# Two 64-row halves of the matmul array side by side in a fused attention and gated-MLP kernel

## The chip, the core and the metric

The kernel runs on one core of one Trainium2 chip. The metric is the device time of one execution in microseconds (us). Three executions of the kernel before gave 696.16, 697.24 and 698.26 us; their median is 697.24 us.

## The reference

```
xn  = layernorm(x)                                   # x: 2048 x 448
out = x + A(xn) @ wo + (sigmoid(xn @ w_gate) * (xn @ w_up)) @ w_down    # 448 -> 1792 -> 448
A: 16 heads of 28 channels, 4 segments of 512 tokens; in each segment causal
   softmax(q k^T / sqrt(28)) v, mixed by sigmoid(beta) with a memory
   phi(q) M / phi(q) z, where M and z are summed over the segments before
```

Everything is fp32. The kernel keeps the accuracy by splitting an operand into a high part, rounded to the matmul's format (float32r), and a low part, the remainder, and by adding the products high x high, high x low and low x high.

## The kernel before

The 448 channels are held in chunks of 128 rows: three whole chunks and a tail of 64. `xs[b]` holds the normalised tokens of block b (512 tokens) as seven slices of 128 partitions by 512 tokens: slices 0 to 2 the high parts of the three whole chunks, 4 to 6 their low parts, and slice 3 the tail, the 64 channels' high part in partitions 0 to 63 and their low part in partitions 64 to 127. A weight tile has eight slices of the same kind, its slices 3 and 7 holding the tail's high and low parts, each twice. `TERMS` (line 53) lists the eleven pairs of slices whose products make one output: nine for the whole chunks, two for the tail.

A front part (to about 165 us) normalises the tokens and computes keys, queries, values and the memory. Then one long loop does two things at once, and its PE order is written out by hand (`manual_schedule` for PE and SP): generators yield after a few matmuls, and the driver at the end (lines 766 to 779) draws one step of attention for a fixed number of steps of the MLP.

- The MLP (`gated`, line 159) walks over 14 groups f of 128 hidden channels, two at a time, and for each pair over the four token blocks: 56 blocks (f, b). A block computes the gate product and the up product, eleven matmuls of 128x512 each (line 240, output `pgu`), then ACT takes tanh of the gate (line 248, output `sg`), DVE multiplies it with the up product (line 249), ACT writes the high half of the result (line 251, `hh`) and DVE the low half (line 252). Between these, the down products of the block two steps back (`down`, line 161, output `pd`) are issued for two tiles of 128 tokens, six matmuls of 448 columns each (line 166), and DVE adds them to `acc` (line 169).
- Attention works on 32 pairs of heads. `scores` (line 588) makes for each pair five PSUM banks of scores (line 597, output `st`), one attention step each; the rows of an operand are 84, three times 28, since the high and low parts are stacked. ACT copies each bank to `w` in SBUF (lines 601 and 604), POOL masks the diagonal tiles (line 612), DVE takes maxima (lines 614 and 618, output `mx`). `weights` (line 624) then finishes a pair: small DVE maxima and POOL copies between partitions (lines 628 to 638), a DVE transpose that spreads the maximum (line 641, `mb`), and three times a DVE subtraction (line 651) and an ACT exponential (line 652). After two pairs, `finish` multiplies the weights with the values (line 672, output `pa`, 128x32 tiles) and DVE normalises (lines 675 to 678).

The eight PSUM banks have tags (line 113): two `p`, two `s`, one `m`, two `gu`, one `pd`. The gate product uses `gu`, the up product `p`, the down products `pd` and `gu` in turn, the scores `s` in turn. A product that opens a bank has to wait until the engine that read the bank's last content is done. The order on ACT, DVE and POOL in this loop is not written by hand: the framework's scheduler lays it out when the program is built, and each of these engines then works strictly through its list.

Of the kernel before, what the change touches and what calls it, by code (L numbers as in the profile page):

```python
# [2 lines left out]

# [6 lines left out]
F32 = mybir.dt.float32  # L10
# [28 lines left out]
SLOT = (0, 0, 0, None, 0, 0, 2, 3, 1, 1, 1, None, 1, 1)  # L39
# [14 lines left out]
KS = 3 * DH  # L54
# [7 lines left out]
def kernel(  # L62
# [96 lines left out]
    def gated():  # L159

        def down(b, hs, wd, t, tag="pd"):
            tok = slice(t * P, (t + 1) * P)
            mms = [(h[:, a, tok], wd[f][:, w, :]) for f, h in hs for a, w in ((0, 0), (0, 1), (1, 0))]
            pd = bank("pd", tag)
            for n, (l, r) in enumerate(mms):
                T.matmul(pd[:, :D], l, r, start=n == 0, stop=n == len(mms) - 1)  # L166
                if n == 2:
                    yield
            V.tensor_add(acc[b][:, t, :], pd[:, :D], acc[b][:, t, :])  # L169
            yield  # L170
# [37 lines left out]
        todo = [None, None]  # L208
        for f0 in range(0, NF, FG):
# [22 lines left out]
            for b in range(NB):  # L232
                hs = []
                for f in range(f0, f0 + FG):
                    pgu = []
                    for side in range(2):
                        slot = 2 * (f - f0) + side
                        dst = bank("pgu", ("gu", "p")[side])
                        for n, (a, w) in enumerate(TERMS):
                            T.matmul(dst, wgu[f][:, w, side * P:(side + 1) * P], xs[b][:, a, :],  # L240
                                     start=n == 0, stop=n == len(TERMS) - 1)
                            if n in (3, 7):
                                yield
                        pgu.append(dst)
# [10 lines left out]
                        yield  # L255
                        if todo and f0 + b > 0:
                            yield from todo.pop(0) or ()
# [3 lines left out]
                todo += [down(b, hs, wdn, t, ("pd", "s" if end else "gu")[t % 2]) for t in range(NT)]  # L261
        rest.extend(todo)
# [305 lines left out]
    class Pair:  # L568
# [5 lines left out]
        def load(self):  # L574

            self.qk = sb.tile([P, 2, 2, L], F32R, name="qk2", bufs=2)
            for c, parts in enumerate(((0, 0), (1, 0), (0, 1))):
                for n in range(2):
                    r0 = D * (1 - n) + DH * self.h0
                    nc.sync.dma_start(self.qk[DH * c:DH * (c + 1), n].bitcast(F32),  # L580
                                      qd[self.s][r0:r0 + 2 * DH, parts[n], :].rearrange("(j p) f -> p j f", p=DH))
# [6 lines left out]
        def scores(self):  # L588
# [4 lines left out]
            for n in range(5):  # L593
                st = bank("st", "s")
                for h, kb in (((n // 2, 0),), ((n // 2, 1), (n // 2, 3)))[n % 2] if n < 4 else ((0, 2), (1, 2)):
                    at = KB[kb] % L + (256 * h if kb == 2 else 0)
                    T.matmul(st[:, at:at + L - kb * P], self.qk[:KS, 1, h, kb * P:(kb + 1) * P],  # L597
                             self.qk[:KS, 0, h, kb * P:], start=True, stop=True)
                if n < 4:
                    w = self.w[:, HW * (n // 2) + L * (n % 2):][:, :L]  # L600
                    A.activation(w, st, AF.Copy)  # L601
                else:
                    w = w3[:, :, 2 * L:]
                    A.activation(w, st.rearrange("p (h n) -> p h n", h=2), AF.Copy)

                if n % 2 == 0 and n < 4:
                    d = w[:, :P]
                    pattern = [[1, P]]
                else:
                    d = w.rearrange("p (a n) -> p a n", n=P)[:, 0:4:3, :] if n < 4 else w[:, :, :P]  # L610
                    pattern = [[0, 2], [1, P]]
                G.affine_select(d, d, pattern=pattern, base=0, channel_multiplier=-1, compare_op=ALU.is_ge, fill=MASK)  # L612
                if n in (1, 3):
                    V.tensor_reduce(mx[:, 16 * (n - 1):16 * (n + 1)],  # L614
                                    w3[:, n // 2, :2 * L].rearrange("p (b n) -> p b n", n=32),
                                    axis=mybir.AxisListType.X, op=ALU.max, apply_transpose=True)
                if n == 4:
                    V.tensor_reduce(mx[:, 64:80].rearrange("p (h b) -> p h b", h=2),
                                    w.rearrange("p h (b n) -> p h b n", n=32),
                                    axis=mybir.AxisListType.X, op=ALU.max, apply_transpose=True)  # L620
                yield
# [112 lines left out]
    def project():  # L734
# [11 lines left out]
        for n in range(NB * NT + 2):  # L746
# [5 lines left out]
            if n >= 2:  # L752
# [10 lines left out]
                if rest:  # L763
                    yield from rest.pop(0)
# [54 lines left out]
```

## Time and profile before

| | |
|---|---|
| median of three runs | 697.24 us |
| the profiled execution's own time | 699.29 us |
| its span, first to last instruction | 697.6 us |
| PE busy | 690.0 us (99%), 3594 matmuls |
| DVE busy | 570.2 us (82%) |
| ACT busy | 343.6 us (49%) |
| POOL busy | 148.5 us (21%) |
| mean granted TensorE clock | 0.997 |

PE is the matmul engine and PEld its weight loads, which run beside the matmuls. A duration of a matmul runs from its start to its modelled end and overlaps the next one; what a matmul costs in a row of matmuls is read from the chain that ended last, where a piece is a time and a count. "idle before" names the engine or DMA that a waiting instruction was released by.

### The profile page before, as it was taken

The numbers are of one execution on the slowest core, as the hardware profiler recorded it, in microseconds if no ns is written. First come the engines' busy times: TensorE is split into PE (matmuls) and PEld (weight loads), VectorE is DVE, ScalarE is ACT, GpSimd is POOL, SyncE is SP. The second block draws the span as 40 slices with busy tenths as digits, with TensorE's granted clock in tenths as the row PEclk, the third lists the DMA queues.
The fourth block names the chain that finished last, engine by engine and source line by source line (L and its number), as shares of the span: only waits on it lengthen the run. The fifth ranks groups of instructions, "written<-read, shape, count | busy, mean of one in ns | idle before, by whom it ended". The sixth has DMA issues, their size and how long they took to land.

```text
span 697.6 us, 10438 instructions
## 1 busy us (share of the span) xinstructions
PE 690.0 (99%) x3594; PEld 567.7 (81%) x3594; DVE 570.2 (82%) x994; ACT 343.6 (49%) x563; POOL 148.5 (21%) x349
## 2 busy tenths in 40 slices
PE   8989999999999999999999999999999999999997
PEld 7878878777878787877878778787787878778897
DVE  6665687658789898988898889998898889889863
ACT  5646646344455455543655446455644555446320
POOL 4400010101222131322222222132221322222000
PEclk9999999999999999999999999999999999999999
DMA  7833545687222423234323343324242432333342
GB/s 265 320 130 149 201 185 211 226 300 224 70 77 65 120 86 85 48 113 108 78 58 96 70 128 66 98 56 114 74 108 66 95 70 60 86 94 88 91 152 105
DMA packets 45797, 84.37 MB, mean 121 GB/s; under 512 B 6321, under 2 KB 20401, under 8 KB 45233
## 3 DMA queue, kind: packets, MB, share of 16 engines
q1 hardware_dynamic: 42736, 76.37, 35.3%
q0 software_dynamic: 3008, 7.34, 5.2%
q8 instruction: 28, 0.46, 0.3%
q14 instruction: 25, 0.20, 0.1%
HBM read 51.05 MB, written 32.64 MB: 120 GB/s over the span
## 4 chain that ended last, share of the span: by engine, by line
PE 94%; DMA 2%; DVE 1%; ACT 1%; SPq 0%; issue 0%; ACTq 0%
PE pgu L240 42%; PE pd L166 20%; PE pp L344 9%; PE st L597 5%; PE pa L672 5%; PE po L756 5%; PE pv L326 4%; PE pmm L372 2%; PE n L390 1%; DMA qd<-qk 1%; DMA acc<-in_x 1%; PE pt L95 1%; PE pk L364 1%; DVE stats L285 0%; ACT L512 0%
## 5 line engine op out<-in xcount | busy, mean ns | idle before, releaser
L240 PE MATMUL pgu<-xs,wgu 128*128 128x512 f32 x1232 | 321.0, 398 | 0.0
L240 PEld LDWEIGHTS pgu<-xs,wgu 128*128 128x128 f32 x1232 | 226.6, 188 | 48.0 <-issue 3.2
L166 PE MATMUL pd<-wdn,hh 128*128 128x448 f32 x672 | 162.4, 368 | 0.0
L612 POOL TENSOR_SCALAR_AFFINE_SELECT w<-w 128x256 f32<-128x256 f32 (+1 forms) x160 | 81.7, 512 | 254.1 <-ACT w L601 215.1
L166 PEld LDWEIGHTS pd<-wdn,hh 128*128 128x128 f32 x672 | 123.2, 188 | 15.1 <-issue 1.0
L652 ACT ACTIVATE w<-w 128x1024 f32<-128x1024 f32 (+1 forms) x96 | 87.1, 915 | 87.6 <-DVE w L651 87.0
L651 DVE TENSOR_TENSOR w<-w,mb 128x1024 f32<-128x1024 f32 (+1 forms) x96 | 99.7, 1049 | 0.2
L601 ACT ACTIVATE w<-st 128x512 f32<-128x512 f32 x128 | 75.0, 588 | 43.6 <-PE st L597 43.5
L614 DVE TRANSPOSE_TENSOR_REDUCE mx<-w 128x32 f32<-128x1024 f32 x64 | 79.1, 1235 | 12.7 <-POOL w L612 12.7
L344 PE MATMUL pp<-xs,wqk 128*128 128x512 f32 x308 | 80.6, 412 | 0.0
L344 PEld LDWEIGHTS pp<-xs,wqk 128*128 128x128 f32 x308 | 58.1, 192 | 14.8 <-issue 2.4
L169 DVE TENSOR_TENSOR acc<-pd,acc 128x448 f32<-128x448 f32 x112 | 67.4, 602 | 2.7 <-PE pd L166 2.5
L597 PE MATMUL st<-qk 84*128 84x128 f32 (+3 forms) x256 | 64.0, 311 | 0.0
L251 ACT ACTIVATE hh<-sg 128x512 fp32r<-128x512 f32 x56 | 35.1, 627 | 44.5 <-DVE sg L249 35.0
L597 PEld LDWEIGHTS st<-qk 84*128 84x128 f32 x256 | 48.4, 189 | 8.6 <-ACT w L601 0.2
L248 ACT ACTIVATE sg<-pgu 128x512 f32<-128x512 f32 x56 | 33.3, 594 | 40.1 <-PE pgu L240 40.1
L641 DVE STREAM_TRANSPOSE mb<-top 128x1024 f32<-128x1024 f32 x32 | 39.8, 1242 | 10.3 <-POOL top L638 10.1
L351 DVE TENSOR_TENSOR qk<-pp,qk 128x512 fp32r<-128x512 f32 x28 | 19.3, 688 | 34.6 <-ACT e L349 27.3
L249 DVE SCALAR_TENSOR_TENSOR sg<-sg,pgu 128x512 f32<-128x512 f32 x56 | 37.4, 668 | 4.8 <-PE pgu L240 4.8
L252 DVE SCALAR_TENSOR_TENSOR hh<-sg,hh 128x512 fp32r<-128x512 f32 x56 | 38.6, 690 | 2.7 <-ACT hh L251 2.5
L326 PE MATMUL pv<-wv,xs 128*128 128x448 f32 x176 | 39.7, 377 | 0.3
L672 PE MATMUL pa<-w,vv 128*32 128x128 f32 (+3 forms) x512 | 38.4, 436 | 0.0
(100 smaller groups left out, 639.2 us busy)
## 6 DMA issues: line engine op xcount, KB each, us to landing
qk<-qd SPq DMA_DIRECT2D x192, 112.0 KB
qd<-qk SPq DMA_DIRECT2D x28, 512.0 KB
raw<-in_w_ffn SPq DMA_DIRECT2D x14, 512.0 KB
vd<-vst SPq DMA_DIRECT2D x4, 1024.0 KB
vv<-vd SPq DMA_DIRECT2D x16, 256.0 KB
od<-w POOLq DMA_DIRECT2D x16, 256.0 KB, 4.0
sums<-od SPq DMA_DIRECT2D x32, 128.0 KB
out<-acc SPq DMA_DIRECT2D x16, 224.0 KB
```

What stands on the lines that cost most here:

```text
L166: T.matmul(pd[:, :D], l, r, start=n == 0, stop=n == len(mms) - 1)
L169: V.tensor_add(acc[b][:, t, :], pd[:, :D], acc[b][:, t, :])
L240: T.matmul(dst, wgu[f][:, w, side * P:(side + 1) * P], xs[b][:, a, :], start=n == 0, stop=n == len(TERMS) - 1)
L326: T.matmul(pv[:, :D], xs[b][:, a, t * P:(t + 1) * P], wv[w], start=n == 0, stop=n == len(TERMS) - 1)
L344: T.matmul(pp, wqk[c][:, w, :], xs[b][:, a, :], start=n == 0, stop=n == len(TERMS) - 1)
L597: T.matmul(st[:, at:at + L - kb * P], self.qk[:KS, 1, h, kb * P:(kb + 1) * P], self.qk[:KS, 0, h, kb * P:], start=True, stop=True)
L601: A.activation(w, st, AF.Copy)
L612: G.affine_select(d, d, pattern=pattern, base=0, channel_multiplier=-1, compare_op=ALU.is_ge, fill=MASK)
L614: V.tensor_reduce(mx[:, 16 * (n - 1):16 * (n + 1)], w3[:, n // 2, :2 * L].rearrange("p (b n) -> p b n", n=32), axis=mybir.AxisListType.X, ...
L651: V.tensor_sub(w, w, m)
L652: A.activation(w, w, AF.Exp, scale=SCALE)
L672: T.matmul(pa[32 * j:32 * j + 32, kb * P:], self.vv[:, kb, 32 * j:32 * j + 32], self.pairs[j // 2].block(j % 2, kb), start=kb == 0, stop=k ...
```

## The change

All products of the loop use the array as two tiles of 64 rows by 128 columns. The new helper `half_by_half` takes two outputs in two PSUM banks. In a first way, rows 0 to 63 add to output 0 and rows 64 to 127 to output 1, one matmul of each in turn; in a second way the outputs change places. Before the second way stands a `keepalive_nop` on PE that names both outputs, so PE waits for the first way's last matmuls to have finished. Other work is issued between the two ways.

```diff
+HALF = [slice(0, 64), slice(64, P)]
+CROSS = [t for c in range(3) for t in ((c, c), (c, 4 + c), (4 + c, c))]
+EARLIER, LATER = slice(0, L // 2), slice(L // 2, L)
+ENDS = [[(EARLIER, 3, 3), (LATER, 3, 3), (EARLIER, 3, 7)], [(LATER, 3, 3), (EARLIER, 3, 3), (LATER, 3, 7)]]
+KS = 3 * DH // 2
...
-        V.tensor_sub(dst[64:, 3, tok], p3[64:, 3], dst[64:, 3, tok].bitcast(F32))
+        low = HALF[1 - t // 2]
+        V.tensor_sub(dst[low, 3, tok], p3[low, 3], dst[low, 3, tok].bitcast(F32))
...
+    def half_by_half(outs, steps, part):
+        for way in range(2):
+            todo = [steps((r + way) % 2, r) for r in range(2)]
+            count = max(len(s) for s in todo)
+            for n in range(count):
+                for r in range(2):
+                    if n < len(todo[r]):
+                        cols, stationary, moving = todo[r][n]
+                        T.matmul(outs[(r + way) % 2][:, cols], stationary, moving, start=way == 0 and n == 0,
+                                 stop=way == 1 and n == len(todo[r]) - 1)
+                if n % part == part - 1 and n < count - 1:
+                    yield
+            yield
+            if way == 0:
+                T.keepalive_nop([T.lower_ap(o[0:1, 0:1]) for o in outs])
...
+            if halves:
+                pds = [bank("pd", t) for t in ("pd", tag)]
+                mms = half_by_half(pds, lambda o, r: steps(o, HALF[r]), 3)
+                for n in range(4):
+                    next(mms)
+                    if n == 3:
+                        add(0)
+                        add(1)
                     yield
...
+        def gate_up(f, xb, pgu):
+            def steps(o, r):
+                return [(tok, wgu[f][HALF[r], w, o * P:(o + 1) * P], xb[HALF[r], a, tok])
+                        for tok, a, w in [(slice(None), a, w) for a, w in CROSS] + ENDS[r]]
+            yield from half_by_half(pgu, steps, 4)
...
-            for n in range(5):
-                st = bank("st", "s")
...
+            for n, kbs in enumerate(((0,), (1, 3), (2,))):
+                st = [bank("st", "s") for _ in range(2)]
...
+                mms = half_by_half(st, steps, 2)
+                next(mms)
+                yield
+                next(mms)
+                w = w3[:, :, L * n:min(L * (n + 1), HW)]
+                for h in range(2):
+                    A.activation(w[:, h], st[h][:, :w.shape[2]], AF.Copy)
```

The tail changes with it: in the second half of a block's 512 tokens the low part now lies in partitions 0 to 63 and the high part in 64 to 127. So each half of the array needs three tail products of 256 columns per output (`ENDS`) where two of 512 columns on all rows stood. Per output and way there are nine products of 512 columns and three of 256.

Gate and up products of a block now run as one unit: both outputs in the first way, then two steps of the down products (their first way), then the second way, then two steps of the down products (their second way). The two tiles of 128 tokens of a down product are made together, and both adds follow at the end. Three of the 56 blocks, the first three, and the last three pairs of down tiles keep the old form. The scores of both heads of a pair are made together: three groups of two banks (512; 384 and 128; 256 columns), each in two ways, each way an attention step; a pair so has six steps instead of five and two empty steps of a unit are gone (`SLOT`). ACT copies two banks per group, 192 copies instead of 160, and POOL has 128 masks instead of 160. The operands of the scores are loaded as 28 and 14 rows into each half of the partitions, by eight DMAs per pair instead of six (256 instead of 192).

The built program has 3263 matmul instructions before and 5533 after. On ACT, DVE and POOL the scheduler has laid out the rest anew. On ACT, from the last score copy (L604) of a pair of heads, w_2463, in the before; `L652` are this pair's exponentials, `L248` tanh of a gate, `w_2589` the next pair's scores:

```order
L604 ACTIVATE w_2463<-st_2550 128x2x256
L601 ACTIVATE w_2589<-st_2591 128x512
L601 ACTIVATE w_2589<-st_2612 128x512
L251 ACTIVATE hh_2603<-sg_2600 128x512
L601 ACTIVATE w_2589<-st_2634 128x512
L248 ACTIVATE sg_2681<-pgu_2627 128x512
L652 ACTIVATE w_2463<-w_2463 128x2x512
L652 ACTIVATE w_2463<-w_2463 128x2x2x256
```

Between a pair's last score copy and its first exponential stood five entries: three score copies of the next pair, an `hh` and a tanh. The same place of the same pair (the sixth) on ACT in the after; `L678` are score copies, `L725` exponentials, `L313` tanh:

```order
L678 ACTIVATE w_2861<-st_2982 128x256
L678 ACTIVATE w_2861<-st_2981 128x256
L725 ACTIVATE w_2861<-w_2861 128x2x512
L725 ACTIVATE w_2861<-w_2861 128x2x2x256
L313 ACTIVATE sg_3067<-pgu_2963 128x512
L725 ACTIVATE w_2861<-w_2861 128x2x2x128
L678 ACTIVATE w_3053<-st_3056 128x512
```

The exponentials now follow the score copies at once, and the next tanh and score copies stand behind them. On DVE at the same place before, from the last of that pair's small maxima to its second subtraction (L651); `L249` and `L252` belong to the MLP, `L169` is an add of down products:

```order
L636 TENSOR_TENSOR top_2582<-mx_2464,up_2581 32x32
L641 STREAM_TRANSPOSE mb_2610<-top_2582 128x1024
L249 SCALAR_TENSOR_TENSOR sg_2600<-sg_2600,pgu_2569 128x512
L169 TENSOR_TENSOR acc0_69<-pd_2606,acc0_69 128x448
L614 TENSOR_REDUCE mx_2590<-w_2589 128x32
L252 SCALAR_TENSOR_TENSOR hh_2603<-sg_2600,hh_2603 128x512
L651 TENSOR_TENSOR w_2463<-w_2463,mb_2610 128x2x512
L651 TENSOR_TENSOR w_2463<-w_2463,mb_2610 128x2x2x256
```

And on DVE in the after (`L691` the last maximum, `L714` the transpose, `L724` the subtractions, `L314` the multiplication with the up product):

```order
L691 TENSOR_REDUCE mx_2862<-w_2861 128x16
L703 TENSOR_TENSOR mx_2862<-mx_2862 128x2x8
L707 TENSOR_TENSOR mx_2862<-mx_2862,up_3045 64x2x16
L709 TENSOR_TENSOR top_3046<-mx_2862,up_3045 32x32
L714 STREAM_TRANSPOSE mb_3080<-top_3046 128x1024
L724 TENSOR_TENSOR w_2861<-w_2861,mb_3080 128x2x512
L724 TENSOR_TENSOR w_2861<-w_2861,mb_3080 128x2x2x256
L724 TENSOR_TENSOR w_2861<-w_2861,mb_3080 128x2x2x128
L314 SCALAR_TENSOR_TENSOR sg_3067<-sg_3067,pgu_2964 128x512
```

The MLP's entries that stood between the transpose and the subtractions have moved behind them. On PE in the after, from the last score products of that pair to the gate product that opens the bank which the tanh above reads (the row of eight is its beginning; a count of two is one matmul on each half):

```order
L129 MATMUL st<-qk_2552 128x256 x2
L129 MATMUL pd<-wdn,hh 128x448 x6
L129 MATMUL pgu<-xs_67,wgu 128x512 x16
L129 MATMUL st<-qk_2749 128x512 x2
L129 MATMUL pgu<-xs_67,wgu 128x512 x2
L129 MATMUL pgu<-xs_67,wgu 128x256 x6
L129 MATMUL pd<-wdn,hh 128x448 x6
L129 MATMUL st<-qk_2749 128x512 x2
L129 MATMUL pd<-wdn,hh 128x448 x6
L129 MATMUL pgu<-xs_67,wgu 128x512 x8
```

On PE in the before, from the same pair's last score products on:

```order
L597 MATMUL st<-qk_2253 128x256 x2
L166 MATMUL pd<-wdn,hh 128x448 x3
L240 MATMUL pgu<-xs_67,wgu 128x512 x8
L597 MATMUL st<-qk_2383 128x512
L240 MATMUL pgu<-xs_67,wgu 128x512 x3
L166 MATMUL pd<-wdn,hh 128x448 x3
L597 MATMUL st<-qk_2383 128x384
L597 MATMUL st<-qk_2383 128x128
L166 MATMUL pd<-wdn,hh 128x448 x3
L240 MATMUL pgu<-xs_67,wgu 128x512 x4
```

Before, groups of scores used the two `s` banks in turn; now both banks of a group are opened, read and opened again together, and the same holds for the `pd` and `gu` banks of a pair of down tiles.

More of the change, by code (lines that the diff above doesn't have):

```diff
@@ L254, in gated @@
                             hs.append((f, hh))
-                        yield
-                        if todo and f0 + b > 0:
-                            yield from todo.pop(0) or ()
+                        if between:
+                            for _ in range(2):
+                                next(between)
+                                yield
+                        else:
+                            yield
                         if (b, slot) in ahead:
@@ L260, in gated @@
                 end = f0 + FG == NF and b == NB - 1
[L261 to L262 removed]
+                todo += [partial(down, b, hs, wdn, t, "s" if end else "gu") for t in (0, 2)]
+        rest.extend(d(False) for d in todo)
     N_FFN = NF // FG * NB * 20 - 12
@@ L763, in project @@
                 if rest:
-                    yield from rest.pop(0)
+                    for _ in range(2):
+                        next(rest[0])
+                        yield
+                    if n % 2 == 1:
+                        rest.pop(0)
     N_OUT = 1 + NB * NT * 3 + 12
```

98 lines of the change are left out of this document (54 added, 44 removed).

## The prediction

> **What bounds the kernel now.** I read the page's busy rows first, then the chain that ended last, then the stretch of the long loop, then who waited for whom.
>
> ```profile
> PE 690.0 (99%) x3594; PEld 567.7 (81%) x3594; DVE 570.2 (82%) x994; ACT 343.6 (49%) x563; POOL 148.5 (21%) x349
> PE pgu L240 42%; PE pd L166 20%; PE pp L344 9%; PE st L597 5%; PE pa L672 5%; PE po L756 5%; PE pv L326 4%; PE pmm L372 2%; PE n L390 1%; DMA qd<-qk 1%; DMA acc<-in_x 1%; PE pt L95 1%; PE pk L364 1%; DVE stats L285 0%; ACT L512 0%
> 170.00:650.00 480.00, 480.00 (x2541) 390.42 (x2540) 426.70 (x686) 248.88 (x390) 123.23 (x304) 1.00 0.33 83
> ```
>
> The third row is the loop, 170 to 650 us: PE is busy in all of its 480.00 us, DVE in 426.70 (89%), ACT in 248.88 (52%). The chain is matmuls after matmuls, so today nothing that DVE, ACT or POOL do is waited for. What a matmul costs in a row of them is read from the chain in order of time, here from 178 to 189 us:
>
> ```profile
> 178.47 0.24 PE st L597 x2
> 178.72 1.63 PE pgu L240 x7
> 180.35 1.23 PE pd L166 x6
> 181.58 2.57 PE pgu L240 x11
> 184.15 0.24 PE st L597
> 184.38 1.22 PE pd L166 x6
> 185.60 0.24 PE st L597 x2
> 185.84 2.62 PE pgu L240 x11
> ```
>
> A 512-column product costs 2.57/11 = 0.233 us, one of 448 columns 1.22/6 = 0.203, two score products of 512 columns together 0.24. No piece of another engine stands between.
>
> The reverse does not hold: the other engines wait for each other.
>
> ```profile
> POOL w L612 <- ACT w L601: 215.1, 95, 5.4
> ACT w L652 <- DVE w L651: 87.0, 57, 6.8
> ```
>
> ACT stood idle for 87.0 us in front of exponentials whose subtraction DVE had not finished, 57 times, once for 6.8 us. Today that delays nobody, since PE needs nothing that is behind them soon. This is the row on which the forecast turns.
>
> **The change: matmul time.** A block's gate and up products shrink from 22 to 21 products' worth: a way has nine pairs of 512 columns and three pairs of 256, so 10.5, and there are two. If a pair of halves costs what one whole product costs, 0.233 us per 512 columns, each of the 53 changed blocks saves 0.233 us: 53 x 0.233 = **12.4 us saved**. Down products and scores stream as many columns as before, so nothing there.
>
> No row shows a 64-row tile. The nearest are the 32-column tiles of the attention's values, four beside each other, against the only whole-array product of the same fp32 kind and length:
>
> ```profile
> L672 PE MATMUL pa<-w,vv 128*32 128x512 f32 x128 | 17.0, 605 | 0.0
> L390 PE MATMUL n<-phi,mst 112*128 112x512 f32 x24 | 12.3, 593 | 0.0
> L672 PE MATMUL pa<-w,vv 128*32 128x128 f32 x128 | 6.8, 273 | 0.0
> ```
>
> A narrow product takes 17.0/128 = 0.133 us of the engine, a whole one 12.3/24 = 0.51: four tiles do run beside each other. I take the same for two halves, with their two products at 0.233 together. From below: the weight load's 188 ns (next row) would be a pair's bound if all else vanished. From above: two products one after another, 0.466.
>
> ```profile
> L240 PEld LDWEIGHTS pgu<-xs,wgu 128*128 128x128 f32 x1232 | 226.6, 188 | 48.0 <-issue 3.2
> ```
>
> Instructions double: a pair is two loads and two products. The narrow tiles give the nearest rate: 6.8/128 = 0.053 us for a load and a product at 128 columns, so 0.106 for a pair. A 512 pair needs 0.233 and a 256 pair 0.117: covered. The 64 score pairs of 128 columns would stream in 0.058: up to 64 x 0.05 = 3 us. Taken 0, upper end 3. The new wait between the ways asks for matmuls that, counted through the order, lie at least twelve half products (1.2 us) back, three times a product's mean 0.40 (L240 row of the page): nothing; queued behind it are all of PE's further products, so if that cover went, a wait would cost about 0.4 us in each of 183 places.
>
> **Edits off the path.** ACT gets 32 score copies more (now 0.59 us each, row below, half as wide), POOL 32 masks fewer: neither is near its bound. The loads of scores' operands go to SP as 64 more DMAs; they are issued when a pair's slot comes free, a whole pair (about 14 us, 32 pairs in the loop's 460) ahead: nothing; without that cover PE's next scores and all behind them would wait for the landing. The subtraction of the tail's low part is as wide as before.
>
> **The change: waits.** Here is the cost. A bank can be opened again only when its reader is done. Before, from a pair's last scores on, PE next needs something that stands behind that pair's second exponential on ACT only 13.9 to 17.5 us later (counted through the orders of all 32 pairs at the durations above). In the after the order on ACT has the exponentials directly behind the score copies, and tanh or the next score copies behind them. For the sixth pair the order on PE shows what lies between: down products 6 half = 0.61 us, gate 16 half = 1.87, scores 0.23, gate 2 and 6 half = 0.58, down 0.61, scores 0.23, down 0.61: 4.74 us. Then comes the product that opens the bank that tanh (L313) reads. What ACT must get through by then is a chain of steps each of which needs the one before. The timeline of one pair in the profile, the fastest of the 32, gives their durations:
>
> ```profile
> 178.31 0.41 PE L597 MATMUL st<-qk 84*128 84x256 f32 x2
> 178.75 0.60 ACT L604 ACTIVATE w<-st 128x512 f32<-128x512 f32 x1 [0.76 <-PE st L597]
> 179.42 0.41 POOL L612 TENSOR_SCALAR_AFFINE_SELECT w<-w 128x256 f32<-128x256 f32 x1 [0.92 <-ACT w L604]
> 179.86 0.71 DVE L618 TRANSPOSE_TENSOR_REDUCE mx<-w 128x16 f32<-128x512 f32 x1
> 181.18 0.21 POOL L633 COPY up<-mx 64x32 f32<-64x32 f32 x1 [1.35 <-DVE mx L630]
> 182.40 0.20 POOL L638 COPY top<-top 64x32 f32<-64x32 f32 x1
> 182.64 1.25 DVE L641 STREAM_TRANSPOSE mb<-top 128x1024 f32<-128x1024 f32 x1
> 183.92 1.23 DVE L651 TENSOR_TENSOR w<-w,mb 128x1024 f32<-128x1024 f32 x1
> 185.66 1.22 DVE L651 TENSOR_TENSOR w<-w,mb 128x1024 f32<-128x1024 f32 x1
> 187.21 1.05 ACT L652 ACTIVATE w<-w 128x1024 f32<-128x1024 f32 x1
> 188.50 0.60 ACT L248 ACTIVATE sg<-pgu 128x512 f32<-128x512 f32 x1 [0.24 <-PE pgu L240]
> ```
>
> From the last score product's end (178.72) to the transpose's start are 3.92 us: copy, mask, maximum, and the exchange between partitions. Then transpose 1.25, subtractions 1.23 and 1.22, the second exponential 1.05, tanh 0.60: 5.35. The sum is 9.27, and 0.17 for the time between the stream's end (178.55, where the next product starts) and the modelled end: **9.4 us** with nothing else between. The cover is 4.7, so PE stands for 4.7 us there. No faster DVE queue helps: it is a chain of dependent steps, and PE's stop also delays the next scores, so the wait comes back with each pair.
>
> Counted the same way through the order, 17 of the 32 pairs have a cover of 4.8 to 6.9 us, on average 5.66, with no or one MLP entry in the chain: 17 x (9.44 - 5.66) = **64.3 us**. The other 15 have 8.0 to 12.3, on average 9.7; in nine of them MLP entries stand inside the chain on DVE (multiply, `hh`, two adds):
>
> ```profile
> L169 DVE TENSOR_TENSOR acc<-pd,acc 128x448 f32<-128x448 f32 x112 | 67.4, 602 | 2.7 <-PE pd L166 2.5
> L601 ACT ACTIVATE w<-st 128x512 f32<-128x512 f32 x128 | 75.0, 588 | 43.6 <-PE st L597 43.5
> L249 DVE SCALAR_TENSOR_TENSOR sg<-sg,pgu 128x512 f32<-128x512 f32 x56 | 37.4, 668 | 4.8 <-PE pgu L240 4.8
> ```
>
> At 0.6 to 0.7 us an entry, three to five of them make the chain 11.4 to 13 and the wait about 2 to 3 us: together some 28 us if all counts, 0 if it hides in POOL's exchange. Taken 14.
>
> The smaller covers: score banks had about 5 us from their last product to their next opening and have 1.25 to 2.3 now. Two copies after each other need at best 0.17 + 0.59 + 0.5 = 1.3 us, more when ACT (52% busy) is at something else. The 64 groups outside the chain above cost between 0 and 0.5 us each; a stop at the chain empties ACT's queue, so I take the low side, 8 us of 0 to 32. The waits of `pd` on DVE's adds (7 us before, about 2.9 now) fall into the same stops: 0.
>
> **The sum.** -12.4 + 64.3 + 14 + 8 = +73.9 us. The profiled execution took 699.29 (span 697.6), 2.05 above the median of 697.24, so I add to the median: **771 us**.
>
> **Rivals.**
>
> *The saving comes through* (faster). ACT and DVE have idle time (48% and 11% of the loop), and before no wait reached PE. If the chain really takes under 5.7 us from scores to second exponential, the short covers hold and the saving remains, less a few small waits: 697.2 - 12.4 + 2 = **687 us**. Against it: in all 32 pairs of the profile the steps above came one after another, and even in the fastest, the one shown, the second exponential ended 9.7 us after the last scores' stream (188.26 less 178.55). Chance 0.13.
>
> *The halves do not run beside each other.* Then the loop's paired products, 53 blocks x 31.5 x 0.233 = 389 us and scores 160 x 0.233 = 37, double; covers double too and the waits vanish: 697 - 12 + 426, about **1110 us**. For it: no row shows 64-row tiles. Against it: four narrow tiles run together at 0.133. Chance 0.04. The Trainium skill, "TensorE: Matmul & The Clock Gate", Part 3, "Measured speedup vs the span model", has row tiles running together; no run here shows it yet.
>
> *The weight loads come free.* In the profile a weight load starts while the product before it still streams (188 ns of load within 233 ns of a product's pace), yet the pace may hold some of the load. If halves freed it fully, a pair would cost 0.188: the 426 us fall by 82, but covers shrink by a fifth as well, 32 x 7.5 x 0.2 = 48 us more waits: 771 - 82 + 48 = **737 us**. Chance 0.05. The Trainium skill, same page, Part 3, "What overlaps and what doesn't", says that weight loads overlap with running matmuls only where the row groups differ. This trace disagrees for today's kernel: with one row group 226.6 us of loads lie beside 321.0 us of products (page, L240) and add no piece to the chain. By that rule the change would gain; by the row it has little to free.
>
> *The waits are half of what I count*, since one stop covers the next and shorter queues shorten the chain: 697.2 - 12.4 + 32 = **717 us**, still slower, inside the forecast's range and counted in its chance; with a little less still the two cancel, so 0.03 for no change.
>
> **How the numbers follow.** The forecast with its bounds has 0.75. Its low end is the half-counted case with nothing else, rounded down: 712. Its high end takes all upper ends: 697.2 - 12.4 + 64.3 + 28 + 32 + 3 = 812, and about 10 for stops of `pd`: 823. Left out are the faster case, no change and the serial halves, 0.20. Three runs lie within 0.15% of their median, so about 0.3% (2 us) is what can be told from no change. Faster 0.13, same 0.03, slower 0.75 + 0.04 + 0.05 = 0.84.
>
> **What would show it.** Right: PE busy falls to about 88% of a longer span; the idle time before gate or score products is released by ACT (tanh, score copies), in stops of 2 to 5 us about once a pair; the chain that ended last now holds DVE and ACT pieces (subtractions, exponentials, transposes); DVE falls to about 74%. A gate product still paces at 0.233 us per pair of halves. Wrong: PE at 98% or more with a shorter span (the saving came through), or a pair at 0.4 us or more without idle time (serial halves), or idle time on PE released by PE's own semaphore (the wait between the ways).

## The result: 860.9 us, 23% slower

The changed kernel takes 860.9 us (median of four runs, 857.61 to 862.28) against 697.75 us of the kernel before beside it: a ratio of 1.2326 (95% interval 1.2299 to 1.2353). The prediction said 771 us and at most 823. The direction, and the place where PE stands, were right; the loss is 163 us where 74 were forecast. The profiled execution took 862.28 us, its span is 860.4.

From the page of the changed kernel: the busy row, the chain that ended last by engine, and the stretch of the loop from 170 to 800 us (busy time of PE, weight loads, DVE, ACT, POOL, then the granted clock, the DMA share and GB/s):

```profile
PE 750.4 (87%) x5864; PEld 632.7 (74%) x5864; DVE 579.1 (67%) x994; ACT 344.6 (40%) x595; POOL 122.9 (14%) x317
PE 34%; DVE 29%; issue 18%; ACT 10%; POOL 5%; DMA 2%; SPq 1%; POOLq 0%; ACTq 0%; DVEq 0%
170.00:800.00 630.00, 532.97 (x4752) 449.36 (x4750) 431.86 (x680) 246.09 (x416) 97.64 (x272) 0.92 0.27 65
```

PE was busy in all of the loop before; now it is idle for 97 of 630 us, and the chain runs through DVE and ACT. DVE and ACT do as much work as before (431.86 and 246.09 us): they are not slower, they are waited for. And the granted clock, 1.00 in the loop before, is 0.92. The waits (us in total, times, longest):

```profile
ACT w L725 <- DVE w L724: 173.7, 41, 6.5
PE st L129 <- ACT w L678: 48.7, 18, 4.6
PE pgu L129 <- ACT sg L313: 30.4, 13, 4.7
PE pd L129 <- DVE acc L198: 19.7, 17, 4.2
```

PE waits for score copies, for tanh and for the adds of the down products. One stop from the timeline (start, duration, engine, line, what; idle time before it and who ended it in brackets):

```profile
401.45 0.40 PE L129 MATMUL st<-qk 42*128 42x512 f32 x2
401.69 1.67 PE L129 MATMUL pgu<-xs,wgu 64*128 64x512 f32 x16
402.32 1.25 DVE L714 STREAM_TRANSPOSE mb<-top 128x1024 f32<-128x1024 f32 x1 [0.57 <-POOL top L711]
403.60 2.96 DVE L724 TENSOR_TENSOR w<-w,mb 128x1024 f32<-128x1024 f32 x3
404.92 2.19 ACT L725 ACTIVATE w<-w 128x1024 f32<-128x1024 f32 x2 [5.96 <-DVE w L724]
407.02 1.06 ACT L678 ACTIVATE w<-st 128x512 f32<-128x512 f32 x2
407.65 1.17 PE L129 MATMUL st<-qk 42*128 42x384 f32 x3 [4.29 <-ACT w L678]
408.73 2.54 PE L129 MATMUL pd<-wdn,hh 64*128 64x448 f32 x11
```

The score copies that PE needs are ready to run at 401.9 us, when their products (the first row) have ended. They stand on ACT behind two exponentials, ACT stands idle for 5.96 us in front of these because DVE has not subtracted yet, and PE stands for 4.29. The last row shows the second half of the bill: eleven half products of 448 columns take 2.54 us, 0.23 each, where they need 0.10 at full clock. Half clock came in 24 spells, nearly all of 3.4 or 6.8 us and 22 of them in the loop, 103 us together by the trace's clock intervals; PE was busy in 91 of these 103 us, so half of the 91, 46 us, were lost. The kernel before loses 1.7 in this way, so 44 belong to the change.

By these numbers the 163 us are: matmuls -12.4 as forecast, waits for ACT +79.1 (48.7 and 30.4), waits for DVE's adds +19.7, half clock +44, and a rest of about 33 us. Little of the rest is in further stops: PE's idle time rose by 102.4 us (110.0 of the span against 7.6), and the three rows hold 98.8 of it. PE's busy time rose by 60.4 us (750.4 against 690.0), which is -12.4, +44 and about 29 more. One part of these 29 can be estimated: a product counts as busy until its modelled end, 0.17 us after its columns have streamed (0.40 less 0.233), and a stop lays this time open; the matmul records show 85 stops in the loop, about half of them under 0.3 us, so 85 x 0.17 = 14 us. Where the other 15 lie was not measured.

### The profile page after: what moved, and what is told of

Same layout as the page of the kernel before. It is cut to its first block, busy times and chain, and to the rows that moved or that the text cites. A ratio compares the mean times of both kernels' runs of the same rounds, so it can differ in the third digit from the quotient of the medians.

```text
span 860.4 us, 15391 instructions
## 1 busy us (share of the span) xinstructions
PE 750.4 (87%) x5864; PEld 632.7 (74%) x5864; DVE 579.1 (67%) x994; ACT 344.6 (40%) x595; POOL 122.9 (14%) x317
## 4 chain that ended last, share of the span: by engine, by line
PE 34%; DVE 29%; issue 18%; ACT 10%; POOL 5%; DMA 2%; SPq 1%; POOLq 0%; ACTq 0%; DVEq 0%
PE pgu L129 11%; DVE w L724 6%; PE pp L412 5%; DVE mx L687 5%; PE pd L129 4%; PE po L829 4%; ACT w L678 4%; DVE mb L714 4%; DVE acc L198 3%; ACT w L725 3%; PE pv L394 3%; DVE mx L691 2%; POOL w L683 2%; PE st L129 2%; DVE sg L314 1%
## 5 line engine op out<-in xcount | busy, mean ns | idle before, releaser
L129 PE MATMUL pgu<-xs,wgu 64*128 64x512 f32 x2544 | 336.1, 392 | 30.4 <-ACT sg L313 30.4
L129 PEld LDWEIGHTS pgu<-xs,wgu 64*128 64x128 f32 x2544 | 284.7, 202 | 61.2 <-ACT sg L313 35.2
L129 PE MATMUL pd<-wdn,hh 64*128 64x448 f32 x1272 | 182.8, 386 | 20.9 <-DVE acc L198 19.7
L129 PEld LDWEIGHTS pd<-wdn,hh 64*128 64x128 f32 x1272 | 133.0, 194 | 34.9 <-DVE acc L198 29.9
L725 ACT ACTIVATE w<-w 128x1024 f32<-128x1024 f32 (+1 forms) x96 | 86.0, 912 | 175.9 <-DVE w L724 173.7
L129 PE MATMUL st<-qk 42*128 42x384 f32 (+3 forms) x512 | 107.6, 349 | 50.0 <-ACT w L678 48.7
L678 ACT ACTIVATE w<-st 128x512 f32<-128x512 f32 (+1 forms) x192 | 90.0, 520 | 123.2 <-PE st L129 100.3
L129 PEld LDWEIGHTS st<-qk 42*128 42x128 f32 x512 | 76.4, 208 | 68.4 <-ACT w L678 64.1
L687 DVE TRANSPOSE_TENSOR_REDUCE mx<-w 128x32 f32<-128x1024 f32 x64 | 75.8, 1223 | 67.7 <-POOL w L683 67.7
L683 POOL TENSOR_SCALAR_AFFINE_SELECT w<-w 128x256 f32<-128x256 f32 x128 | 54.7, 428 | 355.8 <-ACT w L678 353.1
L724 DVE TENSOR_TENSOR w<-w,mb 128x1024 f32<-128x1024 f32 (+1 forms) x96 | 96.3, 1038 | 0.9
L314 DVE SCALAR_TENSOR_TENSOR sg<-sg,pgu 128x512 f32<-128x512 f32 x56 | 37.9, 677 | 56.0 <-ACT sg L313 55.3
L714 DVE STREAM_TRANSPOSE mb<-top 128x1024 f32<-128x1024 f32 x32 | 39.8, 1245 | 17.1 <-POOL top L711 17.0
L313 ACT ACTIVATE sg<-pgu 128x512 f32<-128x512 f32 x56 | 33.2, 593 | 44.0 <-PE pgu L129 40.3
```

The source lines that it names most:

```text
L129: T.matmul(outs[(r + way) % 2][:, cols], stationary, moving, start=way == 0 and n == 0, stop=way == 1 and n == len(todo[r]) - 1)
L314: V.scalar_tensor_tensor(sg, sg, 1.0, pgu[1], op0=ALU.add, op1=ALU.mult)
L678: A.activation(w[:, h], st[h][:, :w.shape[2]], AF.Copy)
L687: V.tensor_reduce(mx[:, 32 * h:32 * (h + 1)], w3[:, h, :2 * L].rearrange("p (b n) -> p b n", n=32), axis=mybir.AxisListType.X, op=ALU.max, ...
L714: V.transpose(mb.rearrange("p h (b n) -> p (h b) n", n=32), top.rearrange("p h b -> p (h b)").unsqueeze(2).to_broadcast([P, 32, 32]))
L724: V.tensor_sub(w, w, m)
```

## The experiments

Theory A, formed on this trace: the halves and the banks opened in pairs cost little; what stops PE is the order in which ACT and DVE go through their lists, which the scheduler laid out anew, and the half clock comes on top of the stops. Against it: the paired banks have too little time whatever the order (B), the halves themselves are slow (C), or, as the prediction had it, the chain of dependent steps is too long (D).

**The order alone.** PE's and SP's order, products and banks as in the changed kernel; a table of numbers sets another order for the entries of ACT, DVE and POOL in the loop, by issue order only, without added waits. It puts first what PE needs first, counted with the profile's durations.

```diff
+ORDER = {
+    mybir.EngineType.Activation: [
+        1, 5, 0, 2, 4, 3, 7, 6, 8, 11, 10, 9, 13, 17, 16, 14, 12, 20, 19, 15, 18, 21, 24, 23, 22, 25, 26, 27,
...
+        for engine, order in ORDER.items():
+            todo = sorted((i for i in nc.cur_bb.bb.instructions if i.engine == engine and
+                           type(i).__name__ != "InstRegisterMove"), key=lambda i: int(i.name[2:]))[-len(order):]
+            for a, b in zip(order, order[1:]):
+                tc.add_manual_dep(todo[b], todo[a].name, mybir.DependencyInfo(
+                    mybir.DependencyClass.NoSync, mybir.DependencyReason.DATA))
```

> The changed kernel with PE's and SP's order untouched: all products in halves, all banks opened in pairs. Only the order of the entries on ACT, DVE and POOL in the loop is another: a table puts first what PE needs first (tanh, score copies, adds of down products), counted with the durations of the profile. Theory A: the stops of PE go, with them the half clock, and the 12.4 us of saved matmul time come through: 683 to 695 us, PE busy 98% or more. Theory B: with the paired banks opened again after 1.25 to 2.3 us the stops stay: 740 us or more. Theory C: as long as the changed kernel, about 860 us, with PE busy and not waiting.

Measured 705.3 us, 1.0103 of before (1.007 to 1.0135). So 155.6 of the 163 us go with the order alone. B and C fall. It is 10 us above A's range; its trace shows a stop of 3.0 us and one of 0.9 with 3.4 us of half clock at the loop's start, where the table had put a weight's split behind a tanh. The second table leaves these first entries as they were:

> The changed kernel with the order of ACT, DVE and POOL in the loop from a table as in the run with its own order (705.3 us), but the first twenty or so entries of the loop left as the scheduler had them: that run had one stop of 3.0 us at 169 us and one of 0.9 behind it, with 3.4 us of half clock, where a weight's split stood behind a tanh. Theory A: these 5 to 6 us go, 698 to 701 us, the time of before. If all of the 12.4 us of saved matmul time were still hidden in stops: 685 to 690 us.

Measured 696.64 us, 0.9983 of before (0.9965 to 1.0002): no difference that could be told. Its busy row and its two largest waits of PE that lie in the loop:

```profile
PE 684.9 (99%) x5864; PEld 582.8 (84%) x5864; DVE 575.0 (83%) x994; ACT 342.9 (49%) x595; POOL 164.6 (24%) x317
PE pd L208 <- DVE acc L277: 0.6, 1, 0.6
PE st L208 <- ACT w L757: 0.6, 1, 0.6
```

At the place on ACT that the change's section shows (the sixth pair, w_2861), the built program's order reads: tanh and two score copies at once, then the exponentials of another pair (w_2588), and this pair's own six entries further on:

```
L757 ACTIVATE w_2861<-st_2982 128x256
L757 ACTIVATE w_2861<-st_2981 128x256
L392 ACTIVATE sg_3067<-pgu_2963 128x512
L757 ACTIVATE w_3053<-st_3056 128x512
L757 ACTIVATE w_3053<-st_3055 128x512
L804 ACTIVATE w_2588<-w_2588 128x2x512
```

**The same table for the kernel before**, laid out in the same way, as a control:

> The kernel before, with the order of ACT, DVE and POOL laid out in the same way as for the changed kernel and held in a table. PE had 2 us of stops in its loop, so no order has much to gain: 695 to 699 us by theory A. If the own order is better in itself, whatever PE waits for, it gains here too: under 690 us.

Measured 696.53 us, 0.9993 (0.9972 to 1.0014). The own order is no gain in itself; it takes away stops where there are some.

**Why the scheduler's order was poor.** The same edit, but with the order that the framework's scheduler itself laid out for a program in which one product stands for each pair of halves:

> The changed kernel with PE's and SP's order untouched. The order on ACT, DVE and POOL is the one that the framework's scheduler laid out for a program with one product in place of each pair of halves, so that PE took in its view the time that a pair takes on the chip; a table holds it. Theory A, with the reason that the scheduler counted a pair as two products after each other and so believed ACT and DVE to have twice the time: most of the loss goes, 725 to 760 us. Rival (the scheduler's order is poor for these banks whatever it believes of PE): 830 us or more.

Measured 751.91 us, 1.0762 (1.07 to 1.0824): two thirds of the loss gone. The stops that are left are short:

```profile
PE st L208 <- ACT w L757: 18.4, 25, 1.6
PE pd L208 <- DVE acc L277: 7.5, 11, 1.6
170.00:690.00 520.00, 488.97 (x4693) 414.63 (x4694) 420.80 (x672) 241.93 (x412) 101.20 (x267) 0.99 0.32 75
```

No stop is over 1.6 us and the clock is 0.99. This fits a scheduler that counts the two halves of a pair one after the other and lays exponentials into time that PE does not give; that the scheduler does so is argued, not shown, since no run shows what it reckons with.

**Order without halves.** The kernel before, ACT and DVE in the order of the program's text:

```diff
-MANUAL = {mybir.EngineType.PE, mybir.EngineType.SP}
+MANUAL = {mybir.EngineType.PE, mybir.EngineType.SP, mybir.EngineType.Activation, mybir.EngineType.DVE}
```

> The kernel before, with ACT and DVE in the order in which the program is written instead of the scheduler's; products, banks and PE's order as before. Theory A: the order alone can cost as much as the change did, since exponentials and maxima then stand ahead of the copies that PE waits for: 800 to 900 us, PE stopped by ACT, with half clock after the stops. If long stops needed the halves or the paired banks: under 730 us.

Measured 857.41 us, 1.228 (1.2229 to 1.233): as much as the change, with whole products and the banks of before, and the same picture (its waits of PE, and 170 to 640 us with the clock at 0.91):

```profile
PE pgu L240 <- ACT sg L248: 50.5, 19, 5.5
PE st L597 <- ACT w L601: 45.7, 25, 3.9
170.00:640.00 470.00, 399.02 (x1881) 310.21 (x1880) 321.38 (x506) 180.82 (x286) 75.20 (x227) 0.91 0.25 64
```

**The chain cut.** The changed kernel with the subtractions working on the spread maximum, so that the exponentials wait for none of the exchange, transpose and subtractions; the scores go into the exponential unshifted, which is the part of the computation left out.

```diff
-                V.tensor_sub(w, w, m)
+                V.tensor_sub(m, m, m)
```

> The changed kernel, but the three subtractions of the maximum work on the spread maximum itself and not on the scores: DVE has the same work in the same shapes, and the exponentials take the scores as they are and wait for no subtraction; the order on ACT, DVE and POOL is laid out anew. The chain from the last scores to the second exponential so loses the exchange, the transpose and the subtractions. Theory A (the order on ACT and DVE): PE is stopped by whatever long entries stand ahead of tanh, score copies and adds, so most stops remain: 810 to 870 us. Theory D (the prediction's: the chain of dependent steps is too long for the cover): ACT is done about 3 us after the last scores, every cover of 4.8 us and more holds, 690 to 725 us.

Measured 848.08 us (two runs). D falls as the cause of the loss: without its chain the kernel is 13 us faster, of 163. Since the order was laid out anew here too, this run alone does not part the chain from the order; the own orders do, with the whole chain and no loss. The waits for ACT have halved, 38.4 us instead of 79.1, and the place has moved to what stands behind DVE's attention work:

```profile
PE pd L129 <- DVE acc L198: 51.2, 30, 4.9
PE st L129 <- ACT w L678: 27.8, 18, 5.3
PE pgu L129 <- ACT sg L313: 10.6, 9, 1.9
```

**Parts of the change.** Only the scores in halves, then only gate, up and down, and then the latter's banks and steps with whole products (the two outputs in turn, no wait between the ways). In short, of the third:

```diff
-                        T.matmul(outs[(r + way) % 2][:, cols], stationary, moving, start=way == 0 and n == 0,
+                        T.matmul(outs[r][:, cols], stationary, moving, start=way == 0 and n == 0,
...
-            if way == 0:
-                T.keepalive_nop([T.lower_ap(o[0:1, 0:1]) for o in outs])
```

> Only the scores are made in halves; gate, up and down products are whole as before, so no matmul time is saved. Theory A (the order in which ACT and DVE work through their lists stops PE, not the halves): from a pair's last scores to the first product that needs something behind its second exponential PE now has 9.2 to 15.5 us of other products in all 32 pairs, against the 9.4 us that the chain needs, so the chain costs about nothing; the two score banks that are opened together leave 64 stops of 0.3 to 0.8 us: 715 to 750 us. Theory B (the banks opened in pairs are too few, whatever the order): the scores' banks are the ones with the least time between two openings, and most of the loss is theirs: 780 us or more. Theory C (the halves themselves run slower than whole products): 160 score products are under a tenth of the matmul time: 700 to 710 us.

> Only gate, up and down products are made in halves; the scores are whole, in five banks as before. 12.4 us of matmul time are saved. Theory A: half of the 32 pairs have 4.9 to 8.8 us of other products between their last scores and the first product that needs something behind the second exponential, against 9.4 us of chain: 50 us of stops there, some 50 more at the adds of the down products and tanh, and on top the half clock that followed each stop of several us in the changed kernel (about 45 us of its 163): 790 to 850 us. Theory B: the score banks are as before, so most of the loss is gone: 700 to 740 us. Theory C: the gate and down products carry the loss: 830 to 860 us, with a pair of halves above 0.233 us.

> The same as the kernel with only gate, up and down products changed: outputs opened in pairs, the same steps between them, both adds at the end. But each product is a whole one on 128 rows, the two outputs taking turns, so nothing is saved and the order that the scheduler lays out on ACT and DVE is laid out beside whole products. Theory A: with the order back near that of before, the paired banks alone cost little: 705 to 730 us. Theory B: the paired banks cost the same as with halves, 790 us or more. Theory C: 697 to 700 us, since no product is a half.

Measured 780.13 us (1.1175, 1.1141 to 1.1209), 861.81 us (1.2367, 1.231 to 1.2424) and 716.58 us (1.0265, 1.0237 to 1.0294). The third is as A expected: paired banks, with an order laid out beside whole products, cost 19 us. The first two missed: together they lose half as much again as the whole change. The first lies on the edge of B's range and the second just above C's, but neither for the reason that B or C gives: PE does not wait for score banks in the one, and a pair of halves is not slow by itself, as is shown below. In the kernel with only the scores in halves PE hardly waits at all; its busy row, and its chain in order of time from 402 us:

```profile
PE 765.8 (99%) x3850; PEld 558.5 (72%) x3850; DVE 574.1 (74%) x994; ACT 344.6 (44%) x595; POOL 127.7 (16%) x317
402.08 0.32 PE st L126 x2
402.40 0.89 PE pgu L266 x3
403.29 0.59 PE pd L192 x3
403.89 0.32 PE st L126 x2
404.20 0.81 PE pd L192 x3
405.01 0.93 PE pgu L266 x4
405.94 0.42 PE st L126 x2
```

The time is in the products: three of 448 columns take 0.81 us behind a score pair and 0.59 behind gate products, a score pair 0.32 to 0.42 where 0.24 is the most that it needs. None of A, B and C had said this; a change between whole products and halves seemed to have a price. It was measured by itself, without the reference's work:

> Not the reference's work: streams of products with nothing to wait for: 96 whole products of 512 columns; 96 pairs of halves; then twelve times 8 whole products and 2 whole ones on 84 rows; twelve times 8 whole ones and 2 pairs of 42-row halves; twelve times 8 pairs on 64 rows and 2 pairs on 42; twelve times 8 pairs and 2 whole ones on 84 rows; and pairs of 448, 512 and 256 columns in turn. Theory A (a change between whole products and halves has its price, and that is what the kernel with only the scores in halves pays in 192 places): 0.4 us for each visit of halves among whole products and of whole ones among halves, nothing for 84 rows among 128 or 42 among 64; a pair at 0.233 us as a whole product. Rival (halves on 42 rows are slow themselves): the visits of 42 rows among 64-row pairs cost as much as among whole products.

Pairs on 42 rows among whole products, then 64-row and 42-row pairs in turn (22 pairs in one row), from the timeline:

```profile
97.33 0.73 PE L95 MATMUL h<-xs 42*128 42x512 f32 x4
97.99 2.12 PE L89 MATMUL whole<-xs 128*128 128x512 f32 x8
100.03 0.73 PE L95 MATMUL h<-xs 42*128 42x512 f32 x4
129.04 5.24 PE L95 MATMUL h<-xs 64*128 64x512 f32 x44
42.85 22.08 PE L95 MATMUL h<-xs 64*128 64x512 f32 x192
```

Two pairs and eight whole products take 100.03 - 97.33 = 2.70 us; ten times 0.233 would be 2.33. A visit of halves among whole products so costs 0.37 us, in round after round, and the same for whole ones among halves (0.37 to 0.40). The 64- and 42-row pairs in turn pay nothing: 22 pairs in 5.24 us with the last one's end. The kernel with only the scores in halves makes 191 such visits: 191 x 0.38 = 73 of its 82 us. The one with only the MLP in halves makes 160: 61 us, with 39 us of half clock, some 70 us of stops and -12.4 about its 164. The changed kernel, all in halves, pays next to none of it. So C is wrong of the halves by themselves; it is the mixture that is slow.

**The clock after a stop**, by itself: streams of 100 whole products with stops between.

> Not the reference's work: 25 streams of whole 512-column products, each some 23 us long, and between them 24 stops in which PE waits for a chain of ACT copies, from 1 to 18 copies of about 0.6 us, rising and then falling. Theory A (the clock follows the stop): after stops of 3 us and more the granted clock is 0.5 for 3.4 or 6.8 us, so each of them costs 1.7 to 3.4 us beyond itself, and after stops under 2.5 us it stays 1.0; a longer stop costs no more than that. Rival (the half clock of the changed kernel came from its many short stops added up, or from the halves): no half clock after any single stop among whole products.

Each row is the stream of 99 products behind the first one; the first has its stop in brackets:

```profile
47.27 0.50 PE L95 MATMUL pa<-gap,xs 128*128 128x512 f32 x1 [1.41 <-ACT gap L93]
47.60 22.62 PE L95 MATMUL pa<-xs 128*128 128x512 f32 x99
99.58 0.50 PE L95 MATMUL pa<-gap,xs 128*128 128x512 f32 x1 [2.73 <-ACT gap L93]
99.91 24.23 PE L95 MATMUL pa<-xs 128*128 128x512 f32 x99
186.37 0.80 PE L95 MATMUL pa<-gap,xs 128*128 128x512 f32 x1 [4.71 <-ACT gap L93]
186.97 25.15 PE L95 MATMUL pa<-xs 128*128 128x512 f32 x99
351.81 0.80 PE L95 MATMUL pa<-gap,xs 128*128 128x512 f32 x1 [11.98 <-ACT gap L93]
352.40 24.41 PE L95 MATMUL pa<-xs 128*128 128x512 f32 x99
```

After stops of 0.75 and 1.41 us (four) the stream takes 22.62 us; after 2.07 us once 22.63 and once 24.21; after every one of the eighteen from 2.73 us on 23.8 to 25.3, and a longer stop is no dearer. So a stop of 2.73 us or more in a stream of products costs 1.4 to 3.0 us beyond itself (with the first product's 0.3). A holds, but for one of the two stops of 2.07 us; the halves and summed stops are not needed for the half clock.

The length of a single stop does not tell all, though. In the kernel with the order for pairs one stop of 1.05 us was followed by half clock 1.6 us later, and in the changed kernel a stop of 2.60 us by none. The first and third row are the products behind these stops; the second and fourth are stretches behind them, with the clock as the third number from the end:

```profile
599.93 0.38 PE L208 MATMUL st<-qk 42*128 42x256 f32 x1 [1.05 <-ACT w L757]
601.55:604.96 3.41, 3.41 (x24) 2.90 (x22) 2.55 (x7) 1.75 (x4) 0.41 (x1) 0.50 0.12 23
488.86 0.93 PE L129 MATMUL st<-qk 42*128 42x384 f32 x3 [2.60 <-ACT w L678]
488.90:492.30 3.40, 3.35 (x31) 3.10 (x33) 1.88 (x2) 2.02 (x4) 0.82 (x1) 1.00 0.03 7
```

Two more spells of that run came after stops of 0.63 and 1.05 us and of 0.99 and 1.05 us close together, and two of the changed kernel's 22 after one stop of 1.19 us and after stops of 0.61 and 1.01 us. So short stops can bring half clock too; when they do was not measured.

**The wait between the ways**, three for one in the kernel with the second own order:

```diff
-                T.keepalive_nop([T.lower_ap(o[0:1, 0:1]) for o in outs])
+                for _ in range(3):
+                    T.keepalive_nop([T.lower_ap(o[0:1, 0:1]) for o in outs])
```

> The changed kernel with its second own order, and three of the waits between the ways in place of each one, all for the same matmuls: 404 more of them on PE. If such a wait costs PE nothing, as the prediction had it, this takes as long as the run with one. If the 202 waits are what eats the saved 12.4 us (0.06 us each), it takes 20 to 28 us longer.

Measured 699.18 us against 696.64, both beside the same before (1.0012, 0.9993 to 1.0031, against 0.9983, 0.9965 to 1.0002): 2.5 us for 404 more waits, about 6 ns each, and the two intervals overlap. The waits that were added are for matmuls that the first of the three has already waited for, so this is the price of a wait that finds its matmuls finished. If all 202 waits do (the prediction counted 183), they cost some 1 us.

## Why the prediction was wrong

**Matmul time: right of the pair, wrong of the saving.** 192 half products stand in 22.08 us, 96 pairs at 0.23 each, as whole products: the halves do run beside each other. The saving of 12.4 us is there in the second own order's trace only in part: its loop, from the first score product to the last of the values, is 484.8 us against 485.6. Against the pace of its products PE loses 38.4 us in this loop and lost 26.9 before, so 11.5 of the 12.4 are eaten, at changes from one kind of product to the next. By the starts of the products, 6.4 us of this lie in eleven pieces of 0.3 to 1.1 us that the loop before does not have; ten of them end with a release by ACT or DVE, so they are short stops that even this order leaves (the two rows of waits shown for it are the idle part of two of them). The other 5 us are in pieces of 0.1 to 0.3 us; what these are was not settled. None of the eleven is ended by the wait between the ways.

**Weight loads: right.** Loads beside running products free nothing: a pair paces like a whole product though its two loads go to different rows. The Trainium skill ("TensorE: Matmul & The Clock Gate", Part 3, "What overlaps and what doesn't") has weight loads overlap with running matmuls only where the row groups differ. These runs do not bear that out: if the loads came free the prediction had a pair at 0.188 us, and here a pair and a whole product both take 0.23.

**The waits: right in place and nearly in size, wrong in reason.** Stops at tanh and score copies were put at 64.3 + 14 + 8 = 86 us and measure 79.1. But "no faster DVE queue helps: it is a chain of dependent steps" failed. With the chain cut, 848 us remain; with the chain whole and another order, 697. Given the scheduler's order the chain does set how long ACT stands (5.96 us in the stop shown), and so the size came out near; but the waits for ACT fall only to 38.4 us without it and to next to nothing with another order. The cover was short because the order put the exponentials ahead of tanh and copies, and the same scheduler had done otherwise beside whole products. The prediction counted a property of the order as one of the work.

**The waits of `pd`: wrong.** Put at nothing ("fall into the same stops"), they measure 19.7 us: adds stand behind runs of attention work on DVE as tanh does on ACT.

**The sum: the step that failed.** It has no term for the clock, neither in its value nor in its upper end. The stops that it forecast, "2 to 5 us about once a pair", are of the length after which PE mostly gets half its clock; this cost 44 us. The Trainium skill has such a cost: "TensorE: Matmul & The Clock Gate", "HAM oscillation — how this bites in real kernels", warns of idle gaps over about 3.4 us and prices the slow stretch that follows at half its length. The clock of 0.5 in the spells here agrees with that price; the stops that bring them can be shorter, in the stream of products 2.73 us always and 2.07 us once of twice, and in one kernel 1.05 us. With the clock's 44 us and the adds' 20 the forecast would have been 835 us, above its range. The remaining 26 us are not in the waits, which were forecast larger than they are; they lie in time in which the trace counts PE as busy, and about half of them stays open. Two bounds of the prediction also do not follow from its sums: the half-counted case is 716.8, not 712, and 812 and 10 are 822; neither matters here.

**Rivals.** "The saving comes through" asked for a chain under 5.7 us; the own order shows that the waits go without a shorter chain, but of the saving only 0.8 us of the loop come through. Serial halves did not happen. "The waits are half" did not either.

**What would show it.** PE at 88% (87%), stops released by ACT, a chain through DVE and ACT and the pair's pace (in the streams by themselves) came as said. DVE at 74% did not: 67%, of a longer span.

## What to carry to other kernels

Where a scheduler lays out ACT and DVE, a change of PE's work is also a change of their order: read the new order for what PE waits for, and try an order that puts first what PE needs first, before calling a wait the price of the change. A stop of PE of 2.7 us or more cost 1.4 to 3.0 us more in half clock, and shorter ones sometimes did too; in the changed kernel 99 us of stops cost 44 more, about half as much again. Halves of the array cost nothing if all of a loop is in halves, and here they gained nothing that could be told; whole products and halves in turn cost 0.37 us a visit.

## What the hardware showed beside this

These are readings of the run with streams of products by themselves. A pair of 64-row halves paces as one whole product at 512 columns (0.23 us), and pairs of 42 rows among pairs of 64 cost nothing, nor do whole products on 84 rows among those on 128 (0.23 us from start to start at each change). Of these changes only the one between whole products and halves has a price, and it is paid on both sides: about half of the 0.37 us at the beginning of a visit of halves, and half at its end.
